# Seven block products in place of eight for five gated groups of a fused attention and mixture-of-experts kernel

## Chip, cores and metric

One core of one Trainium2 chip runs the kernel. The metric is the device time of one execution in microseconds (us), and less is better. The kernel before was run three times: 654.65, 654.56 and 653.83 us, median 654.56 us.

## What is computed

An attention layer with random features gives `x`, 1152 rows (2 batches of 576 tokens) of 512 numbers. A gated layer follows, then four experts. The part that the change touches is the gated layer:

```python
def _moe_ref(x, w1, w2, w3, w_out):
    a = x @ w1                     # (1152, 512) @ (512, 1024)
    b = x @ w2
    h = a * b @ w3                 # (1152, 1024) @ (1024, 1024)
    return (h @ w_out)
```

Python groups this as `((a * b) @ w3) @ w_out`. The kernel multiplies `w3 @ w_out` beforehand (it calls this the fold), so that `a * b` meets a matrix of 1024 by 512. The experts then work on that result. The inputs come as float64, and the result is float32.

## The kernel before

**Numbers.** Float32 factors are kept as a pair of tiles, a rounded high part (`HI`) and the rest (`LO`), in the format fp32r. `split` (line 81) makes the pair: ScalarE copies the high part (line 83), then another engine subtracts it from the source (line 84), VectorE unless `eng` names GpSimd. A product takes three passes, low by high, high by low and high by high (`PASSES`). Float64 words become float32 in `from_f64` (line 111): ScalarE scales the upper words, VectorE shifts the lower ones (line 120) and merges both (line 121).

**x.** It lies transposed in four tiles `xt0` to `xt3` (`xb[kk]`, 128 features each), high and low part, both batches side by side in 1152 columns. Tiles 0 and 1 are the lower half of the features, 2 and 3 the upper half. The last 64 tokens of each batch, the tail, come last (`attend_tail`, line 561).

**Gated groups.** The 1024 columns of w1 and w2 are worked through in eight groups of 128. `load_w12(g)` (line 166) loads both matrices' columns and splits them, the low part by GpSimd. Groups 0 and 1 go batch by batch (`gated`, line 187). Groups 2 to 7 go through `gated_both` (line 215): for each of w1 and w2 and for each third of the 1152 columns, 4 feature tiles times 3 passes add up in one bank of the accumulator memory (line 227), 72 matmuls of 384 columns in a group. ScalarE copies the w1 sums out (line 233), VectorE multiplies them with the w2 sums (line 237), and the product is split into the tiles `hid`.

**The fold.** `fold` (line 269) runs beside the attention. Each of its eight sums is split into high and low when it is done.

**Behind the gated groups.** `expert_input(b)` (line 288) multiplies the eight `hid` tiles of a batch with the folded matrix (line 298), 96 matmuls of 288 columns for each half of a batch. The experts follow. Their first matrix product (`hidden`, line 802) already works with seven block products out of sums made by `combine` (line 730), in the scheme of Strassen and Winograd.

**Order.** Two tables give it, `BESIDE` (line 42) for the work beside the attention and `AFTER` (line 43) for what follows: `w3` loads group 3, `b01` is batch 0 of group 1, `m3` is group 3 of both batches, `c0` the expert input of batch 0. A scheduler takes the priorities from that order and lays down each engine's queue ahead of the run. On the chip every queue is then worked off in its order. SyncE's queue issues the loads, with three buffers for the float64 columns.

## Time and profile before

| | |
|---|---|
| median of three runs | 654.56 us (653.83 to 654.65) |
| the profiled execution | 654.0 us |
| its span, first to last instruction | 652.2 us |
| TensorE busy | 640.9 us, 98% of the span |
| VectorE busy | 458.9 us, 70% |
| ScalarE busy | 415.8 us, 64% |
| GpSimd busy | 122.2 us, 19% |
| groups 3 to 7 on TensorE | 171.7 to 235.1 us |
| expert input of both batches on TensorE | 235.1 to 286.0 us |

In the profile PE is TensorE's matmul, PEld its loading of weights, DVE is VectorE, ACT is ScalarE, POOL is GpSimd. Matmuls overlap in the pipeline, so the pace of a stretch is read from start to start and not from the duration of one. The same holds for VectorE, where an instruction's duration is some 0.08 us longer than the step to the next.

### The profile page before, as it was taken

The page shows a single profiled execution, that of the slowest core. Times are in us where ns is not written, and L with a number is a line of the kernel's source. Part 1 is how long each engine was busy: PE and PEld are TensorE (multiplying, and loading weights), DVE is VectorE, ACT ScalarE, POOL GpSimd, SP SyncE. Part 2 cuts the span into 40 slices and gives each one's busy share as a digit, 9 for nine tenths or more (in the row PEclk, how much of TensorE's full clock was granted, in tenths as well). Part 3 has the DMA queues.
Part 4 walks back from the last instruction along what each step waited for, and adds up shares of the span by engine and source line. Part 5 has one row for each costly group of instructions (what it writes and reads, how often), then busy time and mean ns, then how long its engine had stood idle before and what let it go on. Part 6 is the DMA issues. An engine that isn't in the chain of part 4 may idle for free.

```text
span 652.2 us, 12631 instructions
## 1 busy us (share of the span) xinstructions
PE 640.9 (98%) x4971; PEld 609.3 (93%) x4971; DVE 458.9 (70%) x756; ACT 415.8 (64%) x892; POOL 122.2 (19%) x145
## 2 busy tenths in 40 slices
PE   8998999999999999999999999999999999999997
PEld 6787787799999999999999999999999999999997
DVE  4678987957533261757958968788598679687795
ACT  5899556655522242457768767688677687687750
POOL 2223000133310000000131420430422413304200
PEclk9999999999999999999999999999999999999999
DMA  9978762136200011001244782881773855836824
GB/s 249 353 175 228 168 172 66 34 97 197 64 0 1 1 69 62 1 2 65 94 127 87 111 146 51 159 147 19 149 144 51 150 108 86 141 83 95 173 57 147
DMA packets 58396, 70.61 MB, mean 108 GB/s; under 512 B 8864, under 2 KB 43680, under 8 KB 58336
## 3 DMA queue, kind: packets, MB, share of 16 engines
q1 hardware_dynamic: 44720, 48.79, 25.6%
q0 software_dynamic: 12640, 20.19, 21.1%
q8 instruction: 39, 0.64, 0.4%
q10 hardware_dynamic: 976, 0.82, 0.4%
q14 instruction: 21, 0.17, 0.1%
HBM read 47.24 MB, written 22.54 MB: 107 GB/s over the span
## 4 chain that ended last, share of the span: by engine, by line
PE 88%; ACT 5%; DMA 3%; DVE 2%; issue 1%; SPq 1%; DVEq 0%; ACTq 0%
PE ps_f L828 7%; PE ps_f L913 6%; PE ps_et L828 3%; PE ps_po L828 3%; PE ps_w L828 3%; PE ps_x L828 3%; PE ps_kv L828 3%; PE ps_t L828 3%; PE ps_et L913 3%; PE ps_x L913 3%; PE ps_kv L913 3%; PE ps_w L913 3%; PE ps_t L913 3%; DMA f<-in_moe_w_dram 3%; PE ps_po L913 3%; PE ps_f L227 3%
## 5 line engine op out<-in xcount | busy, mean ns | idle before, releaser
L862 POOL DMA_DIRECT2D out_dram<-o x98 | 82.0, 935 | 352.5 <-DVE o L888 174.0
L84 DVE TENSOR_TENSOR hs<-hd,hs 128x1024 fp32r<-128x1024 f32 x48 | 58.4, 1219 | 0.8 <-ACT hs L83 0.8
L83 ACT ACTIVATE hs<-hd 128x1024 fp32r<-128x1024 f32 x48 | 50.6, 1055 | 7.6 <-PE ps_et L913 2.5
L828 PE MATMUL ps_f<-x,w1e 128*128 128x288 f32 x288 | 46.9, 294 | 0.0
L812 ACT ACTIVATE hd<-hd 128x288 f32<-128x288 f32 x96 | 40.9, 436 | 8.0 <-DVE hd L810 7.4
L724 DVE TENSOR_TENSOR hd<-hd 128x512 f32<-128x512 f32 x64 | 43.9, 686 | 1.5 <-ACT hd L812 0.4
L724 DVE TENSOR_TENSOR raw<-raw 128x512 f32<-128x512 f32 x64 | 43.9, 686 | 0.6
L84 DVE TENSOR_TENSOR w2e<-raw,w2e 128x1024 fp32r<-128x1024 f32 x32 | 38.8, 1218 | 6.1 <-ACT w2e L83 6.0
L913 PE MATMUL ps_f<-w2e,hs 128*128 128x256 f32 x288 | 42.7, 282 | 0.0
L828 PEld LDWEIGHTS ps_f<-x,w1e 128*128 128x128 f32 x288 | 41.1, 188 | 0.2
L913 PEld LDWEIGHTS ps_f<-w2e,hs 128*128 128x128 f32 x288 | 38.2, 191 | 0.1
L83 ACT ACTIVATE w2e<-raw 128x1024 fp32r<-128x1024 f32 x32 | 32.8, 1054 | 6.1 <-DVE raw L724 3.7
L84 POOL TENSOR_TENSOR w<-w12f,w 128x512 fp32r<-128x512 f32 x16 | 21.8, 1378 | 66.9 <-ACT w L83 59.2
L84 DVE TENSOR_TENSOR w1e<-raw,w1e 128x1024 fp32r<-128x1024 f32 x24 | 29.3, 1220 | 4.4 <-ACT w1e L83 4.3
L83 ACT ACTIVATE hid<-a 128x192 fp32r<-128x192 f32 (+2 forms) x32 | 13.4, 440 | 29.1 <-DVE a L237 25.2
L83 ACT ACTIVATE w1e<-raw 128x1024 fp32r<-128x1024 f32 x24 | 25.4, 1058 | 4.6 <-DVE raw L724 2.9
L279 PE MATMUL ps_po<-wo,w3T 128*128 128x512 f32 x96 | 24.1, 399 | 1.7 <-DVE w3T L84 1.7
L381 DVE TENSOR_REDUCE mx<-ps_f 128x4 f32<-128x512 f32 x24 | 16.5, 689 | 12.5 <-PE ps_f L375 11.5
L279 PE MATMUL ps_w<-wo,w3T 128*128 128x512 f32 x96 | 24.5, 400 | 0.6 <-DVE w3T L84 0.6
L885 ACT ACTIVATE o<-ps_f,pr 128x256 f32<-128x256 f32 (+1 forms) x37 | 17.8, 480 | 10.4 <-PE ps_f L913 9.6
L84 DVE TENSOR_TENSOR hid<-a,hid 128x192 fp32r<-128x192 f32 (+2 forms) x32 | 17.5, 563 | 9.0 <-ACT hid L83 9.0
L828 PE MATMUL ps_et<-x,w1e 128*128 128x288 f32 x144 | 23.6, 295 | 0.0
(307 smaller groups left out, 1711.5 us busy)
## 6 DMA issues: line engine op xcount, KB each, us to landing
raw<-in_moe_w_dram SPq DMA_DIRECT2D x32, 512.0 KB, 5.5
out_dram<-o POOLq DMA_DIRECT2D x56, 256.0 KB, 4.7
f<-in_moe_w_dram SPq DMA_DIRECT2D x64, 128.0 KB, 3.6
f<-in_moe_w_dram SPq DMA_DIRECT2D x16, 512.0 KB, 4.3
out_dram<-o POOLq DMA_DIRECT2D x42, 128.0 KB, 5.0
f<-in_moe_w_out_dram SPq DMA_DIRECT2D x8, 512.0 KB, 7.4
vr<-in_v_dram SPq DMA_DIRECT2D x8, 256.0 KB, 5.2
o<-out_dram SPq DMA_DIRECT2D x8, 256.0 KB, 4.8
```

Source lines behind the costliest of these rows:

```text
L83: high = nc.scalar.activation(out=hi, in_=src, func=ACTF.Copy)
L84: low = (eng or nc.vector).tensor_tensor(out=lo, in0=src, in1=hi.bitcast(F32), op=ALU.subtract)
L227: nc.tensor.matmul(out=ps[:, :third], lhsT=w12[w, g][:, x, kk], rhs=xb[kk][:, y, cols[c]], start=(kk == 0 and n == 0), stop=(kk == KD - 1 ...
L279: nc.tensor.matmul(out=sums[m], lhsT=w3T[u][:, a, g * P:(g + 1) * P], rhs=wo[hf * 4 + g][:, c], start=(hf == 0 and n == 0), stop=(hf == 1 ...
L381: top = nc.vector.tensor_reduce(out=mx, in_=pv, op=ALU.max, axis=AX.X, negate=True)
L724: nc.vector.tensor_tensor(out=o, in0=x, in1=y, op=op)
L812: nc.scalar.activation(out=h, in_=src, func=ACTF.Relu)
L828: nc.tensor.matmul(out=ps, lhsT=w1t[a][:, x, kk, g * P:(g + 1) * P], rhs=x2[b, kk][:, y, s], start=(k in "125" and kk == 0 and n == 0), st ...
L862: dma = nc.gpsimd.dma_start(out=out[toks, d], in_=src[rows], **({} if fresh else dict(accum_op=ALU.add))).ins
L885: nc.scalar.activation(out=o, in_=ps, func=ACTF.Copy, scale=pr[:, t, e:e + 1])
L913: nc.tensor.matmul(out=ps, lhsT=t[a][:, x, g, j * P:(j + 1) * P], rhs=w2t[b][:, y, g], start=(k in "15" and g == 0 and n == 0), stop=(k in ...
```

## The change

Groups 3 to 7 (`WINO = 3`) are computed with seven block products. The blocks are: of the weights, w1 and w2 by the two halves of the features; of x, the two halves of the features by the two batches. `ORDER` and `NAMES` give the products for the two column halves X and Y of a batch, 288 columns each. One product is 2 feature tiles times 3 passes, so a group has 2 x 7 x 6 = 84 matmuls of 288 columns. Products add up in three banks for each half, and sums between them are made on the way out (`onto`, line 308 of the new kernel).

- Weights: `load_w12_sums` makes four sums of blocks in place (`place`, on 256 columns, line 176) and splits 512, 256, 512 and 512 columns, the low parts by VectorE. A group takes four of the eight weight tiles where it took two.
- x: `whole` holds two batch-0 blocks and a difference in float32; `sums_of_x` makes T1, T2, T3 and T4 out of them, all on VectorE. T4 is written over the lower half of the features of batch 1.
- Outputs: GpSimd multiplies one of the two gated products in each half (`a<-a`), VectorE does the other sums and products and all low parts.
- The fold's sums are copied out in float32 by VectorE and split late, into the weight tiles that come free (`split_fold`, `s0` and `s1` in `AFTER`).
- `expert_input` of batch 0 opens four banks and goes through the first four `hid` tiles of all four ahead of the other four.
- The pools of the experts are laid in another order, so that weights of the first expert do not lie over the weight tiles.

```diff
-AFTER = 'w2 b01 w3 b10 w4 b11 w5 m2 w6 m3 w7 m4 m5 m6 m7 c0 c1'
+AFTER = 'x0 w2 b01 x1 x2 t1 b10 t123 w3 b11 t123 m2 w4 t123 t9 m3 w5 m4 w6 m5 w7 m6 s0 m7 s1 c0 c1'
+WINO = 3
...
-    w3_p = mctx.enter_context(tc.tile_pool(name="w3", bufs=1, side="right"))
+    w3ctx = mctx.enter_context(ExitStack())
+    w3_p = w3ctx.enter_context(tc.tile_pool(name="w3", bufs=1, side="right"))
...
+    TX_p = cctx.enter_context(tc.tile_pool(name="TX", bufs=3, side="right"))
+    fctx = cctx.enter_context(ExitStack())
+    ft = fctx.enter_context(tc.tile_pool(name="ft", bufs=2, side="right"))
+    w12, hid, wo, w3o, w3s, x2, xf, xs = {}, {}, [], [], [], {}, {}, {}
...
+    turn = [0]
+    ORDER = "X1 Y1 X5 Y5 X6 Y6 X2 X7 Y2 Y7 X3 X4 Y3 Y4".split()
+    NAMES = {
+        "1": ("A11", "B11"), "2": ("A12", "B21"), "3": ("S4", "B22"), "4": ("A22", "T4"), "5": ("S1", "T1"), "6": ("S2", "T2"),
+        "7": ("S3", "T3"),
+    }
...
+    def combine(low, high, x11, x12, x21, x22, first, both):
+
+
+        t = {}
+        a = both(low)
+        t["A11"], t["A12"] = a[0], a[1]
+        t["A22"] = first(x22)
+        place(x22, x21, x22, ALU.add)
+        place(x21, x11, x21, ALU.subtract)
+        a = both(high)
+        t["S3"], t["S1"] = a[0], a[1]
+        place(x11, x22, x11, ALU.subtract)
+        place(x12, x12, x11, ALU.subtract)
+        a = both(low)
+        t["S2"], t["S4"] = a[0], a[1]
+        return t
...
+    def gated_words(g, src):
+
+        src = gated_columns(src, g)
+        if g < EARLY:
+            return next_block("w12f")
+        with ExitStack() as order:
+            with tc.issue_after(pairs[-1].loaded):
+                r = load_f64(cv.tile([P, 512, 2], U32, tag="f64", name="f64", bufs=3), [src])
+            for ins in pairs[-1].split:
+                order.enter_context(tc.issue_after(ins))
+            return from_f64(r, "w12f")
+
     def load_w12(g):

+        if g >= WINO:
+            return load_w12_sums(g)
...
+    def load_w12_sums(g):
+
+        low, high = (gated_words(g, src) for src in (mw1, mw2))
+        (x11, x12), (x21, x22) = ((f[:, :256], f[:, 256:]) for f in (low, high))
+
+        def both(src):
+            t = load_w64(w1_p, src, "w12", nc.vector)
+            return [t[:, :, k * 256:(k + 1) * 256].rearrange("p a (k c) -> p a k c", k=2) for k in range(2)]
+
+        def first(src):
+            t = w1_p.tile([P, 2, 512], F32R, tag=w1_p.name, name="w12")[:, :, :256]
+            split(t[:, HI], t[:, LO], src, eng=nc.vector)
+            return t.rearrange("p a (k c) -> p a k c", k=2)
+
+        w12[g] = combine(low, high, x11, x12, x21, x22, first, both)
+
+    whole = []
+
+    def f32_x(kk, m, x, s=slice(0, S)):
+        return xb[kk][:, x, m * S:(m + 1) * S][:, s].bitcast(F32)
+
+    def difference(kk, s, eng):
+        t = whole[2][:, kk, s]
+        eng.tensor_tensor(out=t, in0=f32_x(kk, 1, HI, s), in1=whole[0][:, kk, s], op=ALU.subtract)
+        eng.tensor_tensor(out=t, in0=t, in1=f32_x(kk, 1, LO, s), op=ALU.add)
+
+    def early_sums_of_x(n):
+
+
+        t = TX_p.tile([P, 2, S], F32, tag="T", name="xw")
+        whole.append(t)
+        for kk in range(2):
+            if n < 2:
+                nc.vector.tensor_tensor(out=t[:, kk], in0=f32_x(2 * n + kk, 0, HI), in1=f32_x(2 * n + kk, 0, LO), op=ALU.add)
+            else:
+                difference(kk, slice(0, MAIN), nc.vector)
+
+    def sums_of_x(raw):
+
+
+        seconds, thirds = (h0_p.tile([P, 2, S], F32, tag=h0_p.name, name="xsum") for _ in range(2))
+        for kk in range(2):
+            difference(kk, slice(MAIN, S), nc.vector)
+            xs["B11", kk], xs["B21", kk], xs["B22", kk] = xb[kk][:, :, :S], xb[kk + 2][:, :, :S], xb[kk + 2][:, :, S:]
+        for kk in range(2):
+            t = seconds[:, kk]
+            nc.vector.tensor_tensor(out=t, in0=f32_x(kk + 2, 1, HI), in1=whole[2][:, kk], op=ALU.subtract)
+            nc.vector.tensor_tensor(out=t, in0=t, in1=f32_x(kk + 2, 1, LO), op=ALU.add)
+            yield
+        for kk in range(2):
+            nc.vector.tensor_tensor(out=thirds[:, kk], in0=seconds[:, kk], in1=whole[0][:, kk], op=ALU.subtract)
+        yield
+        for kk in range(2):
+            t = raw_p.tile([P, 2, 512], F32, tag="raw", name="T4").rearrange("p a c -> p (a c)")[:, :S]
+            nc.vector.tensor_tensor(out=t, in0=whole[1][:, kk], in1=seconds[:, kk], op=ALU.subtract)
+            raw.append(t)
+        yield
+        for n, (name, src) in enumerate((("T1", whole[2]), ("T2", seconds), ("T3", thirds))):
+            for kk in range(2):
+                t = xs[name, kk] = (TX_p if 2 * n + kk > 2 else TY_p).tile([P, 2, S], F32R, tag="T", name="T")
+                split(t[:, HI], t[:, LO], src[:, kk])
+                yield
+
+    def last_sum_of_x(raw):
+
+        for kk in range(2):
+            t = xs["T4", kk] = xb[kk][:, :, S:]
+            split(t[:, HI], t[:, LO], raw[kk])
+
+    def gated_sums(g):
+
+
+        hts = [hidden_tile(b, g) for b in range(B)]
+        tags = ALL_BANKS[0] + ALL_BANKS[1]
+        state = {}, {}
+
+        def new_bank():
+            turn[0] += 1
+            return bank(tags[turn[0] % 8])[:, :HS]
+
+        def keep(tag, src):
+            t = a_p.tile([P, HS], F32, tag="a", name="a", bufs=4) if tag else a_p.tile([P, B * S // 3], F32, tag="a2", name="a", bufs=3)[:, :HS]
+            nc.scalar.activation(out=t, in_=src, func=ACTF.Copy)
+            return t
+
+        def onto(t, src, op=ALU.add, eng=nc.vector):
+            eng.tensor_tensor(out=t, in0=src, in1=t, op=op)
+
+        def put(b, s, t):
+            split(hts[b][:, HI, s], hts[b][:, LO, s], t)
+
+        for o in ORDER:
+            c, k = "XY".index(o[0]), o[1]
+            s = slice(c * HS, (c + 1) * HS)
+            now = state[c]
+            if k in "125":
+                now[k] = new_bank()
+            ps = now["1" if k in "1674" else "5" if k in "53" else "2"]
+            a, b = NAMES[k]
+            for kk in range(2):
+                for n, (x, y) in enumerate(PASSES):
+                    nc.tensor.matmul(
+                        out=ps, lhsT=w12[g][a][:, x, kk], rhs=xs[b, kk][:, y, s],
+                        start=(k in "125" and kk == 0 and n == 0), stop=(k in "234" and kk == 1 and n == 2),
+                        skip_group_check=True,
+                    )
+            if k in "156":
+                now["p" + k] = keep(k != "6", ps)
+            elif k == "2":
+                onto(now["p1"], ps)
+            elif k == "7":
+                onto(now["p5"], ps)
+            elif k == "3":
+                onto(now["p6"], ps)
+                onto(now["p6"], now["p5"], ALU.mult, nc.gpsimd)
+                put(1, s, now["p6"])
+            else:
+                onto(now["p1"], ps, ALU.mult)
+                put(0, s, now["p1"])
+
+    def split_fold(n):
+
+        for t in w3o[4 * n:4 * n + 4]:
+            w3s.append(load_w64(w1_p, t, "w3s", nc.vector))

...
-                    split(ht[:, HI, s], ht[:, LO, s], t)
+                    gone[:] = split(ht[:, HI, s], ht[:, LO, s], t)
+
+    gone = []
...
-                    t = a_p.tile([P, third], F32, tag="a2", name="a", bufs=4)
+                    t = a_p.tile([P, third], F32, tag="a2", name="a", bufs=3)
...
-        wt = cv.tile([P, 2, 512], F32R, tag="w3T", name="w3T", bufs=2)
+        wt = ft.tile([P, 2, 512], F32R, tag="w3T", name="w3T")
...
-                t = w3_p.tile([P, 2, 512], F32R, tag="w3o", name="w3o", bufs=KF)
-                split(t[:, HI], t[:, LO], sums[m])
+                t = w3_p.tile([P, 512], F32, tag="w3o", name="w3o", bufs=KF)
+                nc.vector.tensor_copy(t, sums[m])
                 w3o.append(t)
...
-            for i in range(KD):
+            halves = 2 if b == 0 and c == 0 else 1
+            banks = [bank(ALL_BANKS[c][i]) for i in range(KD)]
+            for i, hf in [(i, hf) for hf in range(halves) for i in range(KD)]:

                 j = i // 2 + i % 2 * (KD // 2)
-                ps = bank(ALL_BANKS[c][i])
-                for kk in range(KF):
+                ps = banks[i]
+                for kk in range(KF * hf // halves, KF * (hf + 1) // halves):
                     for n, (x, y) in enumerate(PASSES):
                         nc.tensor.matmul(
-                            out=ps[:, :HS], lhsT=w3o[kk][:, x, j * P:(j + 1) * P], rhs=hid[b, kk][:, y, s],
+                            out=ps[:, :HS], lhsT=w3s[kk][:, x, j * P:(j + 1) * P], rhs=hid[b, kk][:, y, s],
                             start=(kk == 0 and n == 0), stop=(kk == KF - 1 and n == 2),
                         )
                 p = ps[:, :HS]
+                if hf < halves - 1:
+                    continue
                 if b == 0:
...
+    fctx.close()
+    TY_p = cctx.enter_context(tc.tile_pool(name="TY", bufs=3, reuse_waits="tile", side="right"))
     a_p = cctx.enter_context(tc.tile_pool(name="a", bufs=1, reuse_waits="tile", side="right"))
+    raw_x = []
+    steps = sums_of_x(raw_x)
...
             if s == "c0":
                 cctx.close()
+                w3ctx.close()
                 xq_p = mctx.enter_context(tc.tile_pool(name="xq", bufs=1, reuse_waits="tile", side="right"))
             expert_input(int(s[1]))
+        elif s[0] == "t" and s != "t9":
+            with ExitStack() as order:
+                for ins in gone:
+                    order.enter_context(tc.issue_after(ins))
+                for n in s[1:]:
+                    next(steps)
+        elif s == "t9":
+            last_sum_of_x(raw_x)
+        elif s[0] == "x":
+            with ExitStack() as order:
+                for ins in gone:
+                    order.enter_context(tc.issue_after(ins))
+                early_sums_of_x(int(s[1]))
+        elif s[0] == "s":
+            split_fold(int(s[1]))
         elif s[0] == "m":
-            gated_both(int(s[1]))
+            (gated_both if int(s[1]) < WINO else gated_sums)(int(s[1]))
         else:
             gated(a_p, 4, int(s[1]), int(s[2]), ALL_BANKS[int(s[1])])
```

The moves in the queues, with the names of the build. On VectorE, around the end of the last outputs of group 1 (`gated`) and the first product of group 2 (`a` from `ps_t`, 384 columns). Before:

```order
L120 TENSOR_SCALAR f64e_2360<-f64_2357 128x512
L121 SCALAR_TENSOR_TENSOR w12f_2252<-w12f_2252,f64e_2253 128x512
L120 TENSOR_SCALAR f64e_2370<-f64_2367 128x512
L207 TENSOR_TENSOR a_2206<-ps_po_2209,a_2206 128x288
L84 TENSOR_TENSOR hid_2177<-a_2206,hid_2177 128x288
L121 SCALAR_TENSOR_TENSOR w12f_2359<-w12f_2359,f64e_2360 128x512
L120 TENSOR_SCALAR f64e_2477<-f64_2474 128x512
L121 SCALAR_TENSOR_TENSOR w12f_2369<-w12f_2369,f64e_2370 128x512
L120 TENSOR_SCALAR f64e_2487<-f64_2484 128x512
L237 TENSOR_TENSOR a_2290<-ps_t_2323,a_2290 128x384
```

And now (`xw` and `xsum` are sums of x in float32, `T_2259`, `T_2262` and `T_2265` are the split T1, T1 and T2, `w12_2379` is group 4):

```order
L121 TENSOR_SCALAR f64e_2533<-f64_2530 128x512
L85 TENSOR_TENSOR w12_2379<-w12f_2367,w12_2379 128x512
L85 TENSOR_TENSOR hid_2196<-a_2225,hid_2196 128x288
L272 TENSOR_TENSOR xsum_2088<-xsum_2087,xw_1993 128x576
L276 TENSOR_TENSOR T4_2164<-xw_2079,xsum_2087 128x576
L85 TENSOR_TENSOR T_2259<-xw_2082,T_2259 128x576
L121 TENSOR_SCALAR f64e_2540<-f64_2537 128x512
L85 TENSOR_TENSOR T_2262<-xw_2082,T_2262 128x576
L85 TENSOR_TENSOR T_2265<-xsum_2087,T_2265 128x576
L85 TENSOR_TENSOR xt0_78<-T4_2162,xt0_78 128x576
L85 TENSOR_TENSOR w12_2382<-w12f_2374,w12_2382 128x256
L404 TENSOR_TENSOR a_2298<-ps_t_2331,a_2298 128x384
```

The conversions of later groups' words, which stood here, have given way to sums and splits of x.

On TensorE, from the end of group 2 (`w12_2013`, before `w12_2008`) into group 3. Before:

```order
L227 MATMUL ps_po_2307<-xt1_79,w12_2008 128x384 x3
L227 MATMUL ps_po_2307<-xt2_80,w12_2008 128x384 x3
L227 MATMUL ps_po_2307<-xt3_81,w12_2008 128x384 x3
L227 MATMUL ps_f_2379<-xt0_78,w12_2081 128x384 x3
L227 MATMUL ps_f_2379<-xt1_79,w12_2081 128x384 x3
L227 MATMUL ps_f_2379<-xt2_80,w12_2081 128x384 x3
L227 MATMUL ps_f_2379<-xt3_81,w12_2081 128x384 x3
L227 MATMUL ps_f_2394<-xt0_78,w12_2081 128x384 x3
L227 MATMUL ps_f_2394<-xt1_79,w12_2081 128x384 x3
L227 MATMUL ps_f_2394<-xt2_80,w12_2081 128x384 x3
L227 MATMUL ps_f_2394<-xt3_81,w12_2081 128x384 x3
```

And now (`w12_2180` and `w12_2188` are tiles of group 3, `xt2` and `xt3` the upper half of the features):

```order
L394 MATMUL ps_po_2315<-xt2_80,w12_2013 128x384 x3
L394 MATMUL ps_po_2315<-xt3_81,w12_2013 128x384 x3
L323 MATMUL ps_f_2428<-T_2259,w12_2188 128x288
L323 MATMUL ps_x_2437<-T_2259,w12_2188 128x288
L323 MATMUL ps_et_2462<-xt2_80,w12_2180 128x288 x3
L323 MATMUL ps_et_2462<-xt3_81,w12_2180 128x288 x3
L323 MATMUL ps_w_2477<-xt2_80,w12_2180 128x288 x3
L323 MATMUL ps_w_2477<-xt3_81,w12_2180 128x288 x3
L323 MATMUL ps_f_2428<-T_2259,w12_2188 128x288 x2
L323 MATMUL ps_f_2428<-T_2262,w12_2188 128x288
L323 MATMUL ps_x_2437<-T_2259,w12_2188 128x288 x2
L323 MATMUL ps_x_2437<-T_2262,w12_2188 128x288
```

Group 3 begins with T1, and while T1's second parts are made, a product of x itself stands between.

On GpSimd, from the weights of group 2 on. Before:

```order
L84 TENSOR_TENSOR w12_1998<-w12f_1993,w12_1998 128x512
L84 TENSOR_TENSOR w12_2008<-w12f_2003,w12_2008 128x512
L84 TENSOR_TENSOR w12_2081<-w12f_2076,w12_2081 128x512
L84 TENSOR_TENSOR w12_2091<-w12f_2086,w12_2091 128x512
L84 TENSOR_TENSOR w12_2164<-w12f_2159,w12_2164 128x512
L84 TENSOR_TENSOR w12_2174<-w12f_2169,w12_2174 128x512
L84 TENSOR_TENSOR w12_2247<-w12f_2242,w12_2247 128x512
L84 TENSOR_TENSOR w12_2257<-w12f_2252,w12_2257 128x512
```

And now, from group 1 on:

```order
L85 TENSOR_TENSOR w12_1964<-w12f_1959,w12_1964 128x512
L85 TENSOR_TENSOR w12_1972<-w12f_1967,w12_1972 128x512
L85 TENSOR_TENSOR w12_2003<-w12f_1998,w12_2003 128x512
L85 TENSOR_TENSOR w12_2013<-w12f_2008,w12_2013 128x512
L308 TENSOR_TENSOR a_2452<-a_2435,a_2452 128x288
L308 TENSOR_TENSOR a_2460<-a_2444,a_2460 128x288
L308 TENSOR_TENSOR a_2604<-a_2587,a_2604 128x288
L308 TENSOR_TENSOR a_2612<-a_2596,a_2612 128x288
```

The low parts of groups 3 to 7 are gone from this queue, and ten multiplies of 288 columns stand in it.

## Rows read from the trace of the kernel before

**Rows 1.** The page: its head, and TensorE's line of part 1.

```profile
span 652.2 us, 12631 instructions
...
PE 640.9 (98%) x4971; PEld 609.3 (93%) x4971; DVE 458.9 (70%) x756; ACT 415.8 (64%) x892; POOL 122.2 (19%) x145
```

**Rows 2.** Four stretches: us; PE, PEld, DVE, ACT, POOL busy; PEclk, DMA share, GB/s.

```profile
144.20:156.00 11.80, 11.80 (x87) 11.80 (x86) 11.36 (x29) 6.14 (x15) 2.81 (x2) 1.00 0.84 268
156.00:172.00 16.00, 16.00 (x104) 16.00 (x103) 9.88 (x18) 9.29 (x20) 5.28 (x4) 1.00 0.32 99
172.00:235.00 63.00, 63.00 (x360) 63.00 (x359) 20.61 (x39) 19.03 (x41) 5.46 (x4) 1.00 0.00 1
235.00:286.00 51.00, 51.00 (x387) 51.00 (x386) 27.71 (x53) 20.70 (x42) 0.00 (x0) 1.00 0.12 42
```

**Rows 3.** Waits of TensorE, 120 to 300 us: total, times, longest (all there are).

```profile
PE ps_et L134 <- ACT eq L412: 0.4, 1, 0.4
```

**Rows 4.** Timeline of TensorE: start, us, engine, line, operation, count.

```profile
171.70 4.39 PE L227 MATMUL ps_f<-xt,w 128*128 128x384 f32 x24
...
235.06 3.37 PE L298 MATMUL ps_t<-hid,w3o 128*128 128x288 f32 x24
...
286.75 0.96 PE L828 MATMUL ps_kv<-x,w1e 128*128 128x288 f32 x6
287.55 0.96 PE L828 MATMUL ps_et<-x,w1e 128*128 128x288 f32 x6
288.35 0.96 PE L828 MATMUL ps_f<-x,w1e 128*128 128x288 f32 x6
```

**Rows 5.** Timeline of VectorE: pairs that follow each other without a wait.

```profile
124.81 0.69 DVE L121 SCALAR_TENSOR_TENSOR w12f<-w12f,f64e 128x512 uint32<-128x512 uint32 x1 [0.91 <-ACT w12f L119]
125.42 0.68 DVE L84 TENSOR_TENSOR w3T<-w3t,w3T 128x512 fp32r<-128x512 f32 x1
...
144.70 0.41 DVE L463 TENSOR_TENSOR xs<-ps_x,d 128x256 f32<-128x256 f32 x1
145.03 0.45 DVE L207 TENSOR_TENSOR a<-ps_po,a 128x288 f32<-128x288 f32 x1
...
152.54 0.41 DVE L120 TENSOR_SCALAR f64e<-f 128x512 uint32<-128x512 uint32 x1
152.88 0.44 DVE L207 TENSOR_TENSOR a<-ps_w,a 128x288 f32<-128x288 f32 x1
...
236.41 1.23 DVE L84 TENSOR_TENSOR w1e<-raw,w1e 128x1024 fp32r<-128x1024 f32 x1 [0.59 <-ACT w1e L83]
237.55 0.68 DVE L84 TENSOR_TENSOR w1f<-raw,w1f 128x512 fp32r<-128x512 f32 x1
...
286.59 0.45 DVE L319 TENSOR_TENSOR t<-b,ps_w 128x288 f32<-128x288 f32 x1 [2.17 <-ACT b L318]
286.96 0.45 DVE L320 TENSOR_TENSOR t<-b,t 128x288 f32<-128x288 f32 x1
```

**Rows 6.** Timeline of VectorE, four more instructions.

```profile
128.73 0.68 DVE L84 TENSOR_TENSOR xt<-ps_x,xt 128x512 fp32r<-128x512 f32 x1
...
144.08 0.15 DVE L461 TENSOR_SCALAR d<-ps_x 128x4 f32<-128x4 f32 x1
...
146.97 1.51 DVE L120 TENSOR_SCALAR f64e<-f 128x512 uint32<-128x512 uint32 x1
148.40 1.55 DVE L84 TENSOR_TENSOR hid<-a,hid 128x288 fp32r<-128x288 f32 x1
```

**Rows 7.** GpSimd: two pairs of its timeline, then its group: ns min/median/max.

```profile
127.11 2.84 POOL L84 TENSOR_TENSOR w<-w12f,w 128x512 fp32r<-128x512 f32 x2 [29.26 <-ACT w L83]
...
146.82 2.81 POOL L84 TENSOR_TENSOR w<-w12f,w 128x512 fp32r<-128x512 f32 x2 [2.94 <-ACT w L83]
...
L84 POOL TENSOR_TENSOR w<-w12f,w x16: 1280/1318/1614, 127.1 to 185.3; 128x512 fp32r<-128x512 f32 x16
```

**Rows 8.** Timeline of VectorE: a split's second half behind ScalarE's first.

```profile
181.50 0.56 DVE L84 TENSOR_TENSOR hid<-a,hid 128x384 fp32r<-128x384 f32 x1 [0.59 <-ACT hid L83]
```

More of the change, by code (lines that the diff above doesn't have):

```diff
@@ new lines, in attention_moe_kernel, with place @@
+    fctx = cctx.enter_context(ExitStack())
[7 more added lines that the diff above has]
+    }
+    def place(o, x, y, op):
+        nc.vector.tensor_tensor(out=o, in0=x, in1=y, op=op)
@@ new lines, in parts @@
+    def parts(t, src):
+        split(t[:, HI], t[:, LO], src)
+        return t
[13 more added lines that the diff above has]
+        return t
@@ L166, in load_w12 @@
     def load_w12(g):
+        if g >= WINO:
+            return load_w12_sums(g)
         for w, src in enumerate((mw1, mw2)):
-            src = gated_columns(src, g)
-            with ExitStack() as order:
-                if g < EARLY:
-                    f = next_block("w12f")
-                else:
-                    with tc.issue_after(pairs[-1].loaded):
-                        r = load_f64(cv.tile([P, 512, 2], U32, tag="f64", name="f64", bufs=3), [src])
-                    for ins in pairs[-1].split:
-                        order.enter_context(tc.issue_after(ins))
-                    f = from_f64(r, "w12f")
-                t = load_w64(w1_p, f, "w12", nc.gpsimd)
@@ L241, in gated_both @@
                             s = slice(lo - b * S, hi - b * S)
-                            split(hts[b][:, HI, s], hts[b][:, LO, s], t[:, lo - c * third:hi - c * third])
+                            gone[:] = split(hts[b][:, HI, s], hts[b][:, LO, s], t[:, lo - c * third:hi - c * third])
     w3T = []
@@ L721, in next_bank @@
         return bank(("t", "f", "kv", "et", "f", "x", "w", "po")[turn[0] % 8])
-    def place(o, x, y, op):
-        nc.vector.tensor_tensor(out=o, in0=x, in1=y, op=op)
-    def parts(t, src):
-        split(t[:, HI], t[:, LO], src)
-        return t
-    def combine(low, high, x11, x12, x21, x22, first, both):
-        t = {}
-        a = both(low)
-        t["A11"], t["A12"] = a[0], a[1]
-        t["A22"] = first(x22)
-        place(x22, x21, x22, ALU.add)
-        place(x21, x11, x21, ALU.subtract)
-        a = both(high)
-        t["S3"], t["S1"] = a[0], a[1]
-        place(x11, x22, x11, ALU.subtract)
-        place(x12, x12, x11, ALU.subtract)
-        a = both(low)
-        t["S2"], t["S4"] = a[0], a[1]
-        return t
     def raw_half(pool, src):
@@ L794, in load_w2 @@
         return t
-    ORDER = "X1 Y1 X5 Y5 X6 Y6 X2 X7 Y2 Y7 X3 X4 Y3 Y4".split()
-    NAMES = {
-        "1": ("A11", "B11"), "2": ("A12", "B21"), "3": ("S4", "B22"), "4": ("A22", "T4"), "5": ("S1", "T1"), "6": ("S2", "T2"),
-        "7": ("S3", "T3"),
-    }
     def hidden(w1t, c):
```

11 lines of the change are left out of this document (6 added, 5 removed).

## The prediction

> **What bounds the kernel now.** I read the page first, then the stretches around the change, then TensorE's waits, then the timelines of TensorE, VectorE and GpSimd.
>
> The page shows TensorE busy for 640.9 of 652.2 us [rows 1]. An average says little about one place, so the stretches come next: from 144.2 us, through the gated groups, to the end of the expert input at 286 us, TensorE is busy in every microsecond, at the full granted clock, 1.00, its level of 2.4 GHz [rows 2]. Between 120 and 300 us it waits once, for 0.4 us [rows 3]. In groups 3 to 7, TensorE's work is the time. VectorE's share matters as much, since the change loads that engine: it is busy for 11.36 of 11.8 us, then 9.88 of 16, then only 20.61 of 63 [rows 2]. It is already full where the sums of x are to be made, and has two thirds of its time free where groups 3 to 7 run.
>
> **What TensorE saves.** Groups 3 to 7 stand from 171.70 to 235.06 us [rows 4], 63.4 us for 5 x 72 = 360 matmuls, 176 ns for one of 384 columns. The new ones have 288 columns and come in sixes, and the expert's sixes of that width start 0.80 us apart [rows 4], 133 ns each. 5 x 84 = 420 of them take 56.0 us. The gain is 63.4 - 56.0 = **7.4 us**. The time goes with the columns, and changing the bank after six costs nothing in those rows. The Trainium skill, TensorE: Matmul & The Clock Gate, section "Wait — 56ns, not 53.3ns?", gives columns divided by 2.4 GHz plus about 2.5 ns, a fixed cost that speaks against more matmuls; by that estimate 360 x 162.5 - 420 x 122.5 ns is a gain of 7.0 us. The trace's paces are slower than the page's, and I stay with them.
>
> **What VectorE must do, and when.** Its price is the step to the next start [rows 5]: 0.60 us for 512 columns, 0.33 for 256, 0.34 for a shift of 512 words, 1.14 for 1024, 0.37 for 288. No 576 columns are in the trace; between the rows of 512 and 1024 that makes 0.60 + 64 x 0.54 / 512 = 0.67, and 384 and 192 columns likewise 0.47 and 0.27. The counts are from the new queue.
>
> *First place, T2.* The queue starts on the last tail's sums at 144.08 us [rows 6], a start that hangs on TensorE and stays. From there to T2's first split there are 15 instructions of 576 columns (10.0 us), 12 of 512 (7.2), 16 of 288 (5.9), 6 of 256 (2.0), 4 shifts (1.4) and 14 narrow ones at 0.15 [rows 6] (2.1): 28.6 us. GpSimd still splits group 2's weights there, and two VectorE instructions that started beside such a pair took 1.51 and 1.55 us [rows 6, 7] instead of 0.41 and 0.45 [rows 5], 2.2 us in all. That is 144.1 + 28.6 + 2.2 = 174.9 us. Up to T2's second split it has 3 of 576, 2 of 256, 4 of 384 and 2 of 192 to do, 5.1 us, so 180.0. TensorE ends group 2 at 171.7 plus the six matmuls of group 3 that now stand ahead, 172.5, and wants that split 46 matmuls later, at 178.6. **Wait: 1.4 us.** The tails of x that TensorE needs at 152 to 160 us come 0 to 0.5 us too early or late by the same count; I take them as even.
>
> *Second place, the weights of group 5.* VectorE's next 17.7 us (20 of 288, 8 of 512, 8 of 256, 3 shifts, two of 576, one of 384) end at 197.7 without GpSimd. TensorE wants the last of these sums after 192 matmuls, at 172.5 + 25.5 + 1.4 = 199.4.
>
> What GpSimd adds is not in the trace: its multiplies of 288 columns. Its 512 columns took 1.32 us at the median [rows 7], in proportion 0.74. Beside its pair from 127.11 us on, a VectorE instruction that read the accumulator ran its normal 0.68 us at 128.73 [rows 6, 7], while the two slow ones above read and wrote the ordinary memory. A group costs VectorE 9.8 us: 12 outputs (4.4), 2 shifts, 2 merges and 3 splits of 512, 5 instructions of 256 (5.3). Of these 8 x 0.37 = 3.0 us read the accumulator and are of the spared kind. So a multiply costs between nothing and 1.32 us; I take 0.37, half of 0.74, since those spared instructions and the idle moments fall beside some. The Trainium skill, SBUF — State Buffer, section "Who interferes with whom", speaks against the change here: a VectorE instruction with two SBUF inputs and a GpSimd instruction that reads SBUF exclude each other for the whole instruction. The slow pair agrees with it, 1.1 us lost each. By that rule all ten multiplies could cost 7.4 us, mine cost 3.7.
>
> With four of them the weights come at 199.2 (nothing lost) to 200.7 (1.3 us). **Wait: 0.6 us.**
>
> *Third place, group 7.* 22 of 288, 9 of 512, 10 of 256 and a shift are 17.2 us, with four multiplies 18.7: 217.9 to 219. TensorE needs this after 156 matmuls, 20.7 us, at 220.7. No wait. Behind that VectorE has 16 outputs and the fold's eight splits (8 x 0.60), with no weights of groups left, and 73 matmuls of the expert input that need nothing of group 7 stand ahead in TensorE's queue; they cover 9.7 us.
>
> *Hand-overs.* Every split is ScalarE first, VectorE second; with nothing between, VectorE stood for 0.59 us [rows 8]. In the new queue other work stands between most. ScalarE is half free (19 of 63 us) [rows 2]. Bounds are nothing and 40 such splits (4 of weights and 4 of outputs in each group), 23.6 us; near the first, since a filled queue hardly stood (11.36 of 11.8 us busy) [rows 2], I take **1.0 us**.
>
> *The rest.* Copying the fold's sums whole costs VectorE the same 0.60 as the split's half did, and ScalarE is spared eight halves, both beside TensorE's work. The eight splits come back late, under the 9.7 us above; without that cover they cost 4.8 us. The loads of groups 6 and 7 wait in SyncE's queue behind the first expert's, whose buffers T4 holds until about 177 us; they are wanted 20 us later. The expert input has the same matmuls in another order, and the pools' new places set no earlier wait. Zero; for the reordered first expert no row stands, and I choose 1 us either way.
>
> **Sum.** 7.4 - (1.4 + 0.6 + 1.0) = 4.4 us less than the profiled execution's 654.0 us: 649.6. That execution is 0.6 below the median of the three, 654.56, inside their spread of 0.8; I forecast **649.9 us**.
>
> **Rivals.**
>
> *No wait at all.* VectorE keeps ahead, and the whole 7.4 us is gained: 646.6 us. For it: two thirds free in the old stretch. Against: the count at T2 is late by 1.4 us with no lucky step in it. 0.18.
>
> *Hand-overs eat the gain.* If 12 of the 40 splits stand for 0.59 us, 7.1 us are lost: 653.7 for the profiled execution, 654.0 as a median, no change. For it: VectorE has next to no slack up to group 5. Against: the queue alternates outputs and weights. 0.12.
>
> *VectorE becomes the bound, and it is slower.* Its own work up to group 7's last weights ends at 174.9 + 39.9 = 214.8 us. Behind those weights TensorE has 66 matmuls of group 7 and 384 of the expert input, 450 x 0.133 = 59.9 us, which ended at 286.0 before. So it decides at 226.1 us: 11 us of delay on VectorE lose everything. The eight multiplies of GpSimd before it at 1.32 us, each in VectorE's way in full, are 10.6, and two bare hand-overs in each group 5.9: 231.3, the end at 291.2, and 654.0 + 5.2 = 659.2 us. Against: GpSimd's time should fall with the columns, and ten of its old instructions of 1.32 us leave the same stretch. 0.14. (The Trainium skill, SBUF — State Buffer, in the section cited, has that full block as its rule; whether it comes to it hangs on which engine starts first.)
>
> **Numbers.** My forecast has 0.56, the three rivals 0.18, 0.12 and 0.14. About 0.2% (1.3 us) is what a measurement here can tell from no change. Faster by more than that, below 653.25: 0.56 + 0.18 = 0.74. Within it: 0.12. Slower: 0.14. The range takes in the rival without waits with a little of the reordering, and the one that gains nothing, and leaves out the slow one: 646.3 to 654.6. The likeliest case alone lies at 647.3 to 653.2.
>
> **What would show it.** Right: sixes of the new line at 0.80 us and 420 of them; TensorE waiting 2 to 4 us in all, on VectorE, first at T2 and then at weights of groups 4 to 6; VectorE busy above nine tenths from 144 us to 215; a GpSimd multiply near 0.75 us with VectorE's doubled beside it. Wrong: sixes above 0.85 us, waits over 6 us, or an expert stage that has grown by more than 1 us.

## The result, and the profile after

The changed kernel takes 648.94 us, the median of four runs (648.26 to 649.33), beside 654.61 us for the kernel before in the same comparison (653.83 to 654.87). The ratio is 0.9914, with a 95% interval of 0.9897 to 0.9931. The forecast was 649.9 us, in a range of 646.3 to 654.6, and faster. The number held. Three terms behind it did not: of the 3.0 us of waits forecast in the gated groups 0.6 came; the experts lost 2.0, where the sum had zero; and the stretch ahead of the gated groups gained 0.5, where it had zero too.

The profiled execution took 649.33 us. Its page, head and TensorE's line (as [rows 1]):

```profile
span 647.6 us, 12881 instructions
...
PE 634.7 (98%) x5031; PEld 602.1 (93%) x5031; DVE 501.3 (77%) x857; ACT 427.0 (66%) x925; POOL 119.2 (18%) x145
```

The stretches, in the columns of [rows 2], cut at T1's first matmul (172.96 us), at the last sum of weights of group 7 and at the first expert matmul; then the new matmuls' line alone (PE, PEld, PEclk):

```profile
144.00:156.00 12.00, 12.00 (x89) 12.00 (x88) 12.00 (x31) 4.67 (x14) 0.00 (x0) 1.00 0.29 91
156.00:172.96 16.96, 16.96 (x111) 16.75 (x109) 15.90 (x36) 9.21 (x21) 0.00 (x0) 1.00 0.20 62
172.96:218.06 45.10, 44.76 (x337) 44.52 (x337) 44.76 (x97) 29.05 (x67) 7.71 (x7) 1.00 0.19 60
218.06:279.33 61.27, 61.27 (x465) 61.27 (x463) 39.51 (x77) 27.93 (x60) 3.05 (x3) 1.00 0.11 35
```

```profile
140.00:172.00 32.00, 1.11 (x6) 0.95 (x6) 1.00 0.31 99
172.00:232.00 60.00, 56.09 (x414) 55.29 (x414) 1.00 0.20 63
```

All 420 matmuls are there. VectorE is busy for 72.66 of 74.06 us up to 218.06, fuller than the "above nine tenths" of the forecast, and TensorE still misses only 0.34 us. TensorE's waits, first from T1 to the experts, then in the experts (total, times, longest):

```profile
PE ps_po L323 <- DVE a L308: 0.3, 1, 0.3
```

```profile
PE ps_w L1074 <- ACT hd L973: 1.1, 1, 1.1
PE ps_po L1074 <- ACT hd L973: 0.9, 1, 0.9
PE ps_et L1074 <- DVE hs L85: 0.5, 1, 0.5
```

In the kernel before there were none in the gated groups, and in the experts these two:

```profile
PE ps_po L913 <- ACT o L885: 0.6, 1, 0.6
PE ps_w L913 <- ACT o L885: 0.2, 1, 0.2
```

TensorE's timeline at its landmarks: the first features of the queries, T1's first matmul, the new line at its pace and at its one wait, the first expert matmul, the last six of the kernel:

```profile
9.63 1.13 PE L546 MATMUL ps_f<-om,qT 128*128 128x256 f32 x4 [0.66 <-ACT ek L558]
...
172.96 0.29 PE L323 MATMUL ps_f<-T,w 128*128 128x288 f32 x1
...
195.22 0.96 PE L323 MATMUL ps_po<-xt,w 128*128 128x288 f32 x6
196.02 0.96 PE L323 MATMUL ps_kv<-xt,w 128*128 128x288 f32 x6
196.82 0.96 PE L323 MATMUL ps_t<-xt,w 128*128 128x288 f32 x6
198.12 1.06 PE L323 MATMUL ps_po<-T,w 128*128 128x288 f32 x6 [0.34 <-DVE a L308]
199.02 0.95 PE L323 MATMUL ps_et<-T,w 128*128 128x288 f32 x6
...
279.33 0.96 PE L989 MATMUL ps_t<-x,w1e 128*128 128x288 f32 x6
...
643.34 0.88 PE L1074 MATMUL ps_f<-w2e,hq 128*128 128x256 f32 x6
```

The same landmarks of before (group 3 began at 171.70 [rows 4]):

```profile
8.68 1.13 PE L375 MATMUL ps_f<-om,qT 128*128 128x256 f32 x4
...
285.95 0.96 PE L828 MATMUL ps_f<-x,w1e 128*128 128x288 f32 x6
...
647.98 0.88 PE L913 MATMUL ps_w<-w2e,hq 128*128 128x256 f32 x6
```

The span of 652.2 us becomes 647.6 in three pieces. Up to the start of group 3 it is 0.46 us longer (172.96 less the 0.80 of six matmuls already done, against 171.70). That is the start of this execution, whose first features of the queries come 0.95 us later; from them to group 3 the new kernel takes 162.53 us against 163.02, **0.49 us less**. (The same stretch takes 162.4 to 162.6 us in every run with the change below, and 162.95 in the one without it.) The groups and the expert input are **7.08 us shorter** (107.17 against 114.25). The experts, up to the last six, are **1.98 us longer** (364.01 against 362.03).

### The profile page after: what moved, and what is told of

It is laid out like the page before. It is cut to its first block, busy times and chain, and to the rows that moved or that the text cites. A ratio compares the mean times of both kernels' runs of the same rounds, so it can differ in the third digit from the quotient of the medians.

```text
span 647.6 us, 12881 instructions
## 1 busy us (share of the span) xinstructions
PE 634.7 (98%) x5031; PEld 602.1 (93%) x5031; DVE 501.3 (77%) x857; ACT 427.0 (66%) x925; POOL 119.2 (18%) x145
## 4 chain that ended last, share of the span: by engine, by line
PE 85%; DVE 6%; ACT 4%; DMA 3%; issue 1%; SPq 0%; DVEq 0%; ACTq 0%
PE ps_f L989 7%; PE ps_f L1074 6%; PE ps_x L989 3%; PE ps_et L989 3%; PE ps_po L989 3%; PE ps_w L989 3%; PE ps_t L989 3%; PE ps_kv L989 3%; PE ps_kv L1074 3%; PE ps_w L1074 3%; PE ps_et L1074 3%; PE ps_po L1074 3%; PE ps_t L1074 3%; PE ps_x L1074 3%; PE ps_f L323 2%; PE ps_f L467 2%
## 5 line engine op out<-in xcount | busy, mean ns | idle before, releaser
L973 ACT ACTIVATE hd<-hd 128x288 f32<-128x288 f32 x96 | 41.0, 439 | 10.1 <-DVE hd L971 9.6
L308 POOL TENSOR_TENSOR a<-a 128x288 f32<-128x288 f32 x10 | 10.8, 1080 | 78.6 <-DVE a L308 75.5
L989 PE MATMUL ps_po<-x,w1e 128*128 128x288 f32 x144 | 23.9, 295 | 0.0
L989 PE MATMUL ps_t<-x,w1e 128*128 128x288 f32 x144 | 23.8, 294 | 0.0
```

The lines of the kernel that those rows point to most:

```text
L973: nc.scalar.activation(out=h, in_=src, func=ACTF.Relu)
L989: nc.tensor.matmul(out=ps, lhsT=w1t[a][:, x, kk, g * P:(g + 1) * P], rhs=x2[b, kk][:, y, s], start=(k in "125" and kk == 0 and n == 0), st ...
```

## Experiments

Two lengths are read off each run: the *gated stage*, from T1's first matmul to the first expert matmul (106.37 us in the changed kernel), and the *experts*, from there to the last six (362.03 us before, 364.01 now). They settle more than totals, as the last section shows.

**The place in the ring of banks.** The gated groups take 30 accumulator banks from the counter that the experts go on with, so these start 6 places further round the eight.

```diff
+    turn[0] = 0
     for e in range(NE):
```

> Changed kernel with the counter of the ring of accumulator banks set back to 0 ahead of the experts, where the kernel before also starts. In the changed kernel the gated groups take 6 banks each, 30 in all, and the experts begin 6 places further on. Theory A (the place in the ring): the expert stage, from its first matmul to the end of the span, falls from 368.3 us to the 366.3 of the kernel before, TensorE's waits in it from 2.4 us to under 1.0, the time from 648.9 to about 647.0. Theory B (VectorE, ScalarE or the loads come fuller or later into the experts): the stage stays at 368.3 and the time at 648.9, within 0.7. The gated stage stays the same by both: the first expert matmul at 279.3, within 0.4.

647.82 us (647.62 to 648.46), ratio 0.9905 (0.9891 to 0.9918); gated stage 106.39, experts 363.18. A gain of 0.8 us in the experts, less than half of the 2.0.

The kernel before, with `turn[0] = 6` at the same place:

> Kernel before, with nothing changed but the same counter set to 6 ahead of the experts. Theory A (the place in the ring): the expert stage grows from 366.3 us to about 368.3, with TensorE waits of 2 to 2.5 us in place of 0.8, and the time from 654.6 to about 656.6. Theory B (what the gated groups leave behind on VectorE, ScalarE and the queues of loads): no change, 654.6 within 0.7. The first expert matmul stays at 286.0, within 0.3.

656.14 us (655.61 to 656.58), ratio 1.0031 (1.0019 to 1.0042), slower; the first expert matmul at 286.00, the experts 364.18. Its waits there:

```profile
PE ps_po L913 <- ACT hd L812: 0.9, 1, 0.9
PE ps_x L913 <- ACT hd L812: 0.6, 1, 0.6
PE ps_po L828 <- ACT p L816: 0.5, 1, 0.5
PE ps_et L913 <- DVE hs L84: 0.5, 1, 0.5
```

The loss of the changed kernel (2.0 us, experts 364.0) is here in full (2.15), without any part of the change but the counter. Of the 2784 expert matmuls in TensorE's queue all but 60 then stand where they stand in the changed kernel. Theory A holds for that. But with the counter put back the changed kernel has 1.15 us left over the kernel before, and a wait of 1.1 us on the same Relu (L973, at ps_t). Its queue of expert matmuls then differs from that of before in the first expert only. That this order is the cause of the rest is argued, not shown.

Two more places, 3 and 4:

> Changed kernel with the counter of banks at 3 ahead of the experts. Theory A (the place in the ring sets the order of TensorE's queue in the experts, and with it which bank ScalarE still has to empty): the stretch from the first expert matmul to the last six, 364.0 us at place 6 and 363.2 at place 0, differs from both by some tenths up to 2 us, the gated stage stays (105.8 to 106.4 us from T1's first matmul). As place 3 gives nearly the queue of place 0, 363.2 within 0.5 and a time of about 647.8. Theory B (the place has no part): 364.0.

> Changed kernel with the counter of banks at 4 ahead of the experts, a queue that differs from those of places 0, 3 and 6. Theory A (the place in the ring): the stretch from the first expert matmul to the last six lies between 361.5 and 365.5 us and off 364.0 by more than 0.3; the gated stage stays. Theory B (the place has no part): 364.0 within 0.3.

Place 3: 648.88 us, experts 364.10. My guess of 363.2 missed; by its length alone this run fits Theory B, though its waits are others than at place 6 (four, of 0.2 to 0.6 us). Place 4: 650.77 us, ratio 0.9952 (0.9937 to 0.9968), experts 366.48, with a wait of 1.3 us on ScalarE and six waits in all; off 364.0, as Theory A has it, but outside my span, and 3.3 us worse than place 0. The gated stage was 106.39 both times. At all four places TensorE's queue is the same up to the experts, and differs in them. So one integer that computes nothing moves this kernel by 3 us.

**What the expert waits wait for.** In the changed kernel ScalarE does this ahead of the wait that ends at 305.10 us, and TensorE this:

```profile
302.54 0.41 ACT L973 ACTIVATE hd<-ps_x 128x288 f32<-128x288 f32 x1
302.85 0.62 ACT L84 ACTIVATE hq<-hd 128x512 fp32r<-128x512 f32 x1
303.37 1.05 ACT L84 ACTIVATE hs<-hd 128x1024 fp32r<-128x1024 f32 x1
304.31 0.43 ACT L973 ACTIVATE hd<-hd 128x288 f32<-128x288 f32 x1
304.65 0.40 ACT L973 ACTIVATE hd<-ps_w 128x288 f32<-128x288 f32 x1
```

```profile
302.34 0.95 PE L989 MATMUL ps_w<-x,w1f 128*128 128x288 f32 x6
303.13 0.87 PE L1074 MATMUL ps_x<-w2e,hs 128*128 128x256 f32 x6
305.10 0.98 PE L1074 MATMUL ps_w<-w2e,hs 128*128 128x256 f32 x6 [1.09 <-ACT hd L973]
```

Bank `ps_w` is full at about 303.3, ScalarE empties it at 304.65 to 305.05, behind two splits and another Relu, and TensorE's queue wants that bank next. So I moved these Relus:

```diff
-                put(1, g, 0, ps)
+                nc.vector.tensor_scalar(out=hd[:, GH + g, 0, s], in0=ps, scalar1=0.0, scalar2=None, op0=ALU.max)
```

> Changed kernel, place 6 of the ring, with the Relu that is read straight out of an accumulator bank (one in three of the 96, two in each call of the experts' first product) made by VectorE in place of ScalarE. Theory F (ScalarE empties those banks late, behind the high halves of splits; TensorE waited 1.1 and 0.9 us for them): these two waits go, the stretch from the first expert matmul to the last six falls from 364.0 us to 362.0 to 362.8, time about 647.5. Rival (any shift of work gives another queue, with waits elsewhere; VectorE is as full as ScalarE there): the stretch stays above 363.5, with other waits, or grows. The gated stage stays at 106.4 us by both.

651.18 us, ratio 0.9956 (0.9943 to 0.9968); experts 366.48. Both waits are gone, and others stand there (the four longest):

```profile
PE ps_po L989 <- ACT p L977: 1.3, 1, 1.3
PE ps_x L1074 <- DVE hs L85: 0.8, 1, 0.8
PE ps_t L989 <- ACT o L1046: 0.5, 1, 0.5
PE ps_w L1074 <- DVE o L1049: 0.5, 1, 0.5
```

The rival wins: shift work, and the order laid down ahead of the run changes (more than half of the expert matmuls stand elsewhere in TensorE's queue), and with it the waits.

**Is VectorE really just in time?** Matching the queues with the trace, tile by tile, T1's first tile was complete 1.25 us ahead of TensorE's first T1 matmul, T2's second 0.46, group 4's last sums 0.9, group 5's first 0.2 and its last 0.4, group 7's 1.7. At T1 the slack is larger than it looks: that first matmul reads only the high part, and the low part, which VectorE makes, is read first at 174.81 us, 1.85 us later. To test it, T3's sums are computed four times:

```diff
-        for kk in range(2):
+        for kk in (0, 1) * 4:
             nc.vector.tensor_tensor(out=thirds[:, kk], in0=seconds[:, kk], in1=whole[0][:, kk], op=ALU.subtract)
```

> Changed kernel with the two sums that become T3 computed four times in place of once: six more VectorE instructions of 576 columns, 6 x 0.67 = 4.0 us, in the queue ahead of T1 and T2. Theory C (VectorE is only just in time): T1 was ready 1.3 us and T2's second part 0.5 us ahead of TensorE, so TensorE waits about 2.7 us at T1 or T2 and at most 0.8 more at the weights of groups 4 and 5, the first expert matmul comes 3.0 to 3.5 us later, the time is about 652.2. Rival (VectorE has room, since it showed no wait worth naming): less than 1.0 us later, under 650.0. Second rival: the delay is kept and grows, since VectorE has no time free up to group 7: 4 us or more.

652.95 us (652.79 to 653.64), ratio 0.998 (0.997 to 0.9989); gated stage 110.65, 4.28 longer for 4.0 us put in. The second rival was nearest by the number; its reason is not shown. The six sums did not stay together: one more stands ahead of T1's first split, five in all ahead of T2's second, one behind it. And more than 500 of TensorE's matmuls changed places in its queue, so the 4.28 us are the load's and the new order's together. Counted from the first features, VectorE was done with T2's second split 3.4 us later than in the changed kernel, and with the last weights of group 5 only 1.0 later. What is shown is that VectorE had no 4 us to spare: TensorE waited for group 5's first weights and for T3 (its two longest waits):

```profile
PE ps_et L323 <- DVE w L85: 1.5, 1, 1.5
PE ps_kv L323 <- DVE T L85: 1.1, 1, 1.1
```

**GpSimd's multiplies.** The call loses its `nc.gpsimd`:

```diff
-                onto(now["p6"], now["p5"], ALU.mult, nc.gpsimd)
+                onto(now["p6"], now["p5"], ALU.mult)
```

> Changed kernel with GpSimd's ten gated multiplies given to VectorE. In the changed kernel they took GpSimd 1.08 us each, and the VectorE instructions beside them were about 4.1 us longer in sum, 0.41 each. On VectorE each costs 0.37. Theory C (a multiply on GpSimd costs VectorE what it would cost there): the last sums of weights of group 7 are ready at 218 us within 1.0, TensorE's waits and the time stay within 0.7 of 648.9. Rival (the full lock, 1.08 us each): VectorE is ahead by up to 8 x 0.7 = 5.7 us at group 7's weights, while the time gains no more than the 0.6 us that TensorE waits in these groups. Second rival (GpSimd spares VectorE its work): VectorE is 3 us later at group 7's weights and TensorE waits 1 to 3 us more, time 650 to 652.

648.66 us (647.69 to 650.25), ratio 0.9918 (0.9905 to 0.9932). The gated stage is 105.78 us with no wait at all, 0.6 less. Over the whole stage VectorE is busy for 83.20 us with 183 instructions, against 84.27 with 173 in the changed kernel. So the ten multiplies cost VectorE 3.7 us when it does them itself (10 x 0.37), and about 1 us more when GpSimd does. Theory C's price holds within that 1 us. Its date does not: the last sums of group 7's weights are ready 47.3 us after T1's first matmul, against 45.1, but for 1.9 us of that VectorE stood for TensorE. (Some 400 of TensorE's matmuls stand elsewhere in its queue here too.)

**GpSimd's splits, put back for group 3.**

```diff
-            t = load_w64(w1_p, src, "w12", nc.vector)
+            t = load_w64(w1_p, src, "w12", nc.gpsimd if g == 3 else nc.vector)
```

(The 256-column split stayed on VectorE; three of 512 moved, not four as the expectation says.)

> Changed kernel with the four low parts of group 3's weight sums (three of 512 columns, one of 256) given to GpSimd, which made all low parts of that group before. They lie from 148 to 163 us, where VectorE is full. They cost VectorE 2.1 us. Theory G (a GpSimd instruction beside VectorE costs it up to its own length where the operands are in the ordinary memory: 1.1 us for each of two in the trace of before): VectorE gains 2.1 us and loses between 1.5 and 4, so T1 is ready between 0.6 us earlier and 2 us later against TensorE's end of group 2 than in the changed kernel (1.26 us ahead), and TensorE begins to wait at T2's second part or at the weights of groups 4 and 5 if it is later. Rival (GpSimd's work is free for VectorE): T1 is ready 2.1 us earlier, 3.3 us ahead, no wait up to group 5.

One run, 649.88 us. VectorE was spared 1.8 us, and T1's first tile came with 0.14 us to spare in place of 1.25. TensorE then waited 1.2 us for a copy out by ScalarE; gated stage 107.22. GpSimd's three splits, and the VectorE instructions that met them:

```profile
146.17 1.81 POOL L85 TENSOR_TENSOR w<-w12f,w 128x512 fp32r<-128x512 f32 x1 [2.95 <-ACT w L84]
161.56 2.76 POOL L85 TENSOR_TENSOR w<-w12f,w 128x512 fp32r<-128x512 f32 x2 [13.57 <-ACT w L84]
```

```profile
146.09 2.52 DVE L255 TENSOR_TENSOR xw<-xt 128x576 f32<-128x576 f32 x2
...
163.09 1.85 DVE L268 TENSOR_TENSOR xsum<-xt,xw 128x576 f32<-128x576 f32 x1
```

Without GpSimd the first two took 1.42 us and the other 0.75, so 1.10 us was lost twice: 2.2 us for the 1.8 that were saved. That is 0.4 of the 1.1 us by which T1 came later; 0.3 more VectorE stood for ScalarE, and 0.34 is a shift that this queue puts ahead of T1's split. Theory G holds for the price, and T1 lies in its band. That TensorE's wait comes of it is not shown: it waited for ScalarE, and more than 500 of its matmuls stand elsewhere in its queue.

**How much a group brings.** Block products for groups 5 to 7 alone, `t9` behind `m4`, place 6 of the ring:

```diff
-WINO = 3
+WINO = 5
```

> Changed kernel with block products for groups 5 to 7 alone; groups 3 and 4 as before, x of batch 1 overwritten only behind group 4, the experts start at the same place of the ring (6) as in the changed kernel. Theory D (TensorE's time goes with the columns): each group by block products saves 72 x 0.176 - 84 x 0.133 = 1.5 us, so two fewer give back 3.0 us: the first expert matmul 3.0 us later against the start of group 3, time about 651.5; less any wait that two groups fewer take from VectorE, at most 0.6. Rival (much of the gain is fixed, or lost in waits in each group): under 2.0 us given back, under 650.7.

651.02 us (650.67 to 651.48), ratio 0.9955 (0.9937 to 0.9973). The first expert matmul comes 109.62 us after the start of group 3, without a wait, against 107.17 in the changed kernel, of which 0.6 are its wait. So two groups give back 109.62 - 106.57 = 3.05 us, 1.5 each. Theory D holds: the gain goes with the groups.

**The opening of the expert input.**

```diff
-            halves = 2 if b == 0 and c == 0 else 1
+            halves = 1
```

> Changed kernel with the first column half of batch 0 of the expert input taken bank by bank through all eight tiles, as before, in place of the first four tiles of all four banks first. The late splits of the fold had 9.7 us of such matmuls as cover in the forecast. Theory E (the cover is needed): TensorE, with 12 matmuls only before it wants the fifth tile, waits 1 to 4.8 us on VectorE's splits or on group 7's outputs, time 650 to 653. Rival (VectorE's splits are early enough anyway, the last one at 229 us): within 0.7 of 648.9.

648.69 us (648.36 to 650.49), gated stage 106.40. No new wait: the rival holds, the cover was not needed.

**Both edits that gained**, the counter at 0 and the multiplies on VectorE; then the Relus too:

> Changed kernel with both edits that had gained: the counter of banks back to 0 ahead of the experts, and the ten gated multiplies on VectorE. The two lie in different stages, so the gains should add: gated stage from T1's first matmul 105.8 us (106.4 in the changed kernel), experts 363.2 (364.0), time about 647.3, 7.1 below the kernel before. Rival (the experts' gain hangs on how the gated stage ends): experts 364.0 again, about 648.3.

> The two edits that had gained and the Relu of the banks on VectorE. Theory F: the wait of 1.1 us behind a Relu, which is also there at place 0, goes: experts 362.0 to 362.5 us, gated stage 105.8, time about 646.4, close to the sum of the forecast without any wait, 646.6. Rival: other waits come, experts 363.2 or more, 647.3 or more.

The first run: **647.29 us** (646.77 to 647.7), ratio 0.9899 (0.9883 to 0.9914), the shortest median of all; gated stage 105.77 and experts 363.18, just the two lengths found apart. Its interval overlaps that of the changed kernel; the lengths do not leave it in doubt. With the Relus on VectorE: 649.54 us, experts 365.55, worse again: the rival's case.

## Why the prediction was right, and where it was not

**TensorE's saving (7.4 us): right.** The sixes stand 0.80 us apart. Without waits the stage is 105.78 us plus the six matmuls done before (0.80), 106.58 against 114.25: 7.67 us, a little over the term, which rested on 0.80 rounded. The Trainium skill's figure (TensorE: Matmul & The Clock Gate, "Wait — 56ns, not 53.3ns?") had given 7.0 as an estimate; the trace sides with the pace of the rows.

**T2 (1.4 us): wrong, 0.** The failing step is "GpSimd still splits group 2's weights there", 2.2 us. The pair at 146.82 us [rows 7], beside which that price was read, is group 3's: its first tile is the one that TensorE reads from 171.70 on, where group 3 begins. Group 2's pair is the one before it, at 141.29 us. The change gave group 3's low parts to VectorE, so the pair at 146.82 is gone from GpSimd's queue; group 2's now starts at 140.97 and ends ahead of VectorE's first sum on the tail, as it also did before. The run that put group 3's splits back on GpSimd shows the price return, 1.10 us at 146 us. The rest of the count was good: VectorE started on the tail at 143.76, not 144.08, stood once for 0.96 us, and T2's second split began at 177.71 and was done by 178.46, where 180.0 was forecast. TensorE came to it at 178.92.

Group 2's pair, before and after, and VectorE after:

```profile
141.29 2.59 POOL L84 TENSOR_TENSOR w<-w12f,w 128x512 fp32r<-128x512 f32 x2 [7.19 <-ACT w L83]
```

```profile
140.97 2.60 POOL L85 TENSOR_TENSOR w<-w12f,w 128x512 fp32r<-128x512 f32 x2 [6.41 <-ACT w L84]
```

```profile
161.23 0.46 DVE L372 TENSOR_TENSOR a<-ps_po,a 128x288 f32<-128x288 f32 x1 [0.96 <-ACT a L368]
...
177.71 0.75 DVE L85 TENSOR_TENSOR T<-xsum,T 128x576 fp32r<-128x576 f32 x1
```

**Weights of group 5 (0.6): wrong, and it follows from T2.** They were ready at 198.67 and wanted at 199.02. **Group 7 (none): right**, 218.06 against a forecast of 217.9 to 219.

**Hand-overs (1.0): wrong, 0.** From T1 to 218 us VectorE stood for no split. What came in their place, 0.34 us at 198.12, is a bank that VectorE emptied from 197.62 on, and it was late there because the split of 196.31 had stood 0.61 us for a multiply of GpSimd (rows below). By the count the bank would have been empty 0.16 us before TensorE wanted it.

**GpSimd's multiply: the duration wrong, the price somewhat low.** Forecast were 0.74 us and a cost of 0.37 to VectorE. It took this (ns min/median/max):

```profile
L308 POOL TENSOR_TENSOR a<-a x10: 806/1124/1253, 183.8 to 231.8; 128x288 f32<-128x288 f32 x10
```

Beside one of them a split of 288 columns took 1.06 us, where 0.45 is usual [rows 5]:

```profile
195.93 1.12 POOL L308 TENSOR_TENSOR a<-a 128x288 f32<-128x288 f32 x1 [1.16 <-DVE a L308]
```

```profile
196.31 1.06 DVE L85 TENSOR_TENSOR hid<-a,hid 128x288 fp32r<-128x288 f32 x1
...
197.62 0.45 DVE L308 TENSOR_TENSOR a<-ps_po,a 128x288 f32<-128x288 f32 x1
```

Nine VectorE instructions were longer so, 4.7 us in sum, 0.47 for each of the ten. (The expectation above has 4.1 and 0.41; it leaves out the one at 232.20.) The VectorE multiplies that read the accumulator never were. Each of the nine ended 0.28 to 0.56 us after the multiply beside it, a little less than its own usual step, so it stood until the multiply was done. The Trainium skill's rule (SBUF — State Buffer, "Who interferes with whom") has the loser stand for the whole instruction. The trace agrees on who is hit and who is not, and on the standing to the end. Since GpSimd had begun before the VectorE instruction that it held up, less than its own time was lost: at most 0.62 of 0.81 us to a multiply, 1.10 of 1.28 to a split.

**The fold: right that it costs nothing**, but not for its cover, which the run without it shows not to matter. **The stretch ahead of group 3 (zero): 0.49 us gained.** Between the first features of the queries and group 3 TensorE stands idle for 4.85 us (busy for 157.68 of 162.53), against 5.46 before (157.56 of 163.02). Which part of the change does this was not tested.

**The first expert (0, 1 us either way): wrong.** The experts lost 2.0 us, which the prediction itself had named as a sign against it. I had looked at the first expert's order and never asked what else the two stages share. They share the counter of banks, and the kernel before alone, with that counter moved by 6, loses as much. Why 1.15 us stay with the counter put back is open.

So 7.4 - 3.0 had been forecast, and 7.67 - 0.6 - 2.0 + 0.5 came, 5.6 us, as the medians have it (5.67). The profiled execution shows 4.6, since it began 0.95 us later. The mechanism on TensorE held. That the sum came within 1 us of the median is in part luck: waits put 2.4 us too high and a loss of 2.0 us that was not seen nearly cancel. The rival without waits had the gated groups nearly right. The slow rival was far off: it needed 11 us of delay on VectorE, which came late once, by 0.34.

## What to carry to other kernels

A price read in the old trace belongs to two instructions: before it goes into the sum, name both by their tiles, and look whether both are still in the new queue and still meet. When a stage takes buffers from a ring that a later stage goes on with, put the counter back or try its places, since TensorE's order and its waits hang on it. Where an engine is 98% full and nothing waits on it, ask for its slack tile by tile; here 4 us more work, with the new order that it brought, cost 4.3.
